# Token-pair loads, halved inversions and transposes by DMA in a delta-rule attention and MLP kernel

## The chip, the cores and the metric

The kernel runs on one core of one Trainium2 chip. The metric is the device time of one execution in microseconds (us), as a median over runs. A profile is one execution; its span, from the first to the last instruction, is some 2 us shorter than the time of the same run. Engines: PE is TensorE (PEld its weight loads), DVE is VectorE, ACT is ScalarE, POOL is GpSimd, SP is SyncE, which here only issues DMAs. A run is called slow when it is over 1.5% above the fastest run of the same kernel, and fast otherwise; intervals and ratios use fast runs alone.

## The reference, cut to what matters

Four batches, eight heads, 768 tokens, head width 48. A recurrence over tokens keeps one 48x48 state per batch and head, and its gated readout is the input of an MLP.

```python
k_n = k / (np.linalg.norm(k, axis=-1, keepdims=True) + 1e-06)
for t in range(S):
    readout = einsum('bhd,bhde->bhe', q[:, :, t], state)
    y[:, :, t] = g[:, :, t] * readout
    v_old = einsum('bhde,bhd->bhe', state, kt)
    state = state + bt * einsum('bhd,bhe->bhde', kt, vt - v_old)
...
x = y.transpose(0, 2, 1, 3).reshape(B * S, H * D)        # 3072 x 384
h = x @ w_in                                             # 384 -> 2048
out = (h * sigmoid(beta * h)) @ w_out                    # 2048 -> 384
```

## The kernel before

The tokens are cut into 12 chunks of 64. For each chunk there is a preparation that no other chunk is needed for (scale k, transpose k and q, products of k and q, the inverse of a triangular 64x64 matrix by repeated products), a short chain that needs the state of the chunk before (pW, w, pU, u, pO, S), then the gated output y, its transpose xT, and the MLP on 256 tokens. The program is planned in Python: every piece of work is an operation with a duration and a key, and a list scheduler puts all of them into one fixed order per engine. On the chip the order is kept; an operation whose input is late holds up everything behind it on that engine.

The transposes, all on TensorE, with a copy out of PSUM (the accumulation memory) after each:

```python
def e_tr(e, sl, dst, src):
    ...
    for s in sl:
        for j in range(PAIRS):
            nc.tensor.transpose(pv[:, s, j, :], sv[:, s, j, :], I128b)
...
G.add(f"pk{c}", [("pe", PAIRS * 57.0 * m)], lambda e, sl=sl: e_tr(e, sl, pk, kp), key - 55, ...)
lean(G.add(f"kT{c}", [("dve", ...), ("act", ...)], lambda e, r=r: e_trc(e, r, kq.t[:, 0, r], pk), ...))
... # pq, qT the same for q
def e_pY(e):
    for s in range(2):
        for i in range(KC):
            nc.tensor.transpose(pv[:, i, s, :], yf[:, s, P * i:P * i + P], I128b)
```

The inverse adds the identity on GpSimd (or DVE) before two of its products:

```python
for sl in groups:
    add_eye(f"ni{c}", ni, nn, K - 37, sl)                # ni = nn + I
...
product(f"pG{c}", pG, ni_, in_j(x4), HJ, HR, SR, ...)
```

The MLP takes chunks in groups; those of two chunks use matmuls of 512 columns:

```python
GROUPS = [[0], [1], [2], [3], [4, 5], [6], [7], [8, 9], [10, 11]]
...
nc.tensor.matmul(ph.t[:, width * i:width * i + width], w_in_b[:, dc, P * fb:P * fb + P],
                 xTb[g].t[:, dc, 0:width], start=(dc == 0), stop=(dc == KC - 1))
```

In gaps the planner puts matmuls of zeros ("fillers") to keep TensorE's clock up. They count as busy time in the profile.

## Time and profile before

| | before |
|---|---|
| median time, 3 runs | 246.2 us (245.78 to 246.34) |
| span of the profile, mean granted clock | 246.8 us, 0.978 (its own run took 248.5 us) |
| first MLP matmul, end of the last one | 31.1 us, 241.2 us |
| PE busy | 221.3 us (90%), 264 transposes of k, q and y among 4930 matmuls |
| DMA busy, first 155 us and after | about 0.9 of 16 engines, then 0.1 to 0.2 |

The page of a profile has the busy shares, then 40 equal slices of the span with a digit for the busy tenths of each, then queues and groups of instructions. A line of the timeline reads: start, duration, engine and source line, operation, output and inputs, shape, count, and in brackets the engine's idle time before it and what released it. "issue" in the brackets means that the profile shows no wait.

### The profile page before, as it was taken

The numbers are of one execution on the slowest core, as the hardware profiler recorded it, in microseconds if no ns is written. First come the engines' busy times: TensorE is split into PE (matmuls) and PEld (weight loads), VectorE is DVE, ScalarE is ACT, GpSimd is POOL, SyncE is SP. The second block draws the span as 40 slices with busy tenths as digits, with TensorE's granted clock in tenths as the row PEclk, the third lists the DMA queues.
The fourth block names the chain that finished last, engine by engine and source line by source line (L and its number), as shares of the span: only waits on it lengthen the run. The fifth ranks groups of instructions, "written<-read, shape, count | busy, mean of one in ns | idle before, by whom it ended". The sixth has DMA issues, their size and how long they took to land.

```text
span 246.8 us, 10951 instructions
## 1 busy us (share of the span) xinstructions
PE 221.3 (90%) x4930; PEld 146.1 (59%) x4950; DVE 157.9 (64%) x208; ACT 170.3 (69%) x287; POOL 124.7 (51%) x110
## 2 busy tenths in 40 slices
PE   4778598786899999999999999999999999999990
PEld 4444475475566776766654657767776456654560
DVE  7568967598657898974797468785893965100000
ACT  4564768596466789868699888778866877357510
POOL 2369447899177976498815874999301002000000
PEclk9999979999599999999999999999999999999999
DMA  6999997969956997998999788703002020020222
GB/s 122 161 206 163 214 241 130 294 104 163 152 90 144 155 189 129 150 163 170 159 176 169 141 159 143 151 5 66 3 13 60 3 66 5 0 66 0 64 64 65
DMA packets 107582, 29.12 MB, mean 118 GB/s; under 512 B 100832, under 2 KB 107504, under 8 KB 107536
## 3 DMA queue, kind: packets, MB, share of 16 engines
q1 hardware_dynamic: 104800, 26.55, 60.7%
q0 software_dynamic: 1600, 1.57, 4.1%
q8 instruction: 38, 0.62, 1.2%
q10 hardware_dynamic: 1136, 0.30, 0.7%
q14 instruction: 8, 0.07, 0.1%
HBM read 25.27 MB, written 4.72 MB: 122 GB/s over the span
## 4 chain that ended last, share of the span: by engine, by line
PE 72%; DVE 8%; DMA 5%; POOL 4%; ACT 4%; issue 3%; ACTq 1%; DVEq 0%; POOLq 0%
PE banks L1159 25%; PE banks L1137 24%; PE banks L743 14%; PE banks L799 4%; PE banks L1025 3%; DMA ld<-in_moe_w_out_dram 3%; DVE w_out_b L737 2%; POOL ni L935 2%; DMA ld<-in_k_dram 2%; PE banks L1108 1%; POOL tiny L827 1%; DVE y L1095 1%; ACT kq L761 1%; ACT raw L761 1%; DVE tt L763 1%
## 5 line engine op out<-in xcount | busy, mean ns | idle before, releaser
L1146 ACT ACTIVATE gT<-banks,betac 128x256 bf16<-128x256 f32 (+1 forms) x144 | 70.0, 550 | 18.3 <-PE banks L1137 18.2
L1159 PE MATMUL banks<-w_out_b,gT 128*128 128x384 bf16 x384 | 74.1, 330 | 4.2 <-DVE w_out_b L737 2.9
L1137 PE MATMUL banks<-xT,w_in_b 128*128 128x256 bf16 (+1 forms) x420 | 71.4, 310 | 2.1 <-ACT gT L1146 0.5
L1137 PEld LDWEIGHTS <-w_in_b 128*128 128x128 bf16 x432 | 40.4, 99 | 21.5 <-issue 2.5
L1159 PEld LDWEIGHTS <-gT 128*128 128x128 bf16 x384 | 34.8, 98 | 24.5 <-issue 4.5
L827 POOL TENSOR_TENSOR tiny<-tiny,half 128x16 f32<-128x16 f32 x10 | 29.3, 2931 | 7.1 <-DVE tiny L820 7.0
L909 DVE TENSOR_TENSOR xa<-banks,UA 128x1024 bf16<-128x1024 f32 x22 | 26.1, 1217 | 4.6 <-PE banks L743 4.5
L763 POOL CAST s<-S_f 64x768 bf16<-64x768 f32 x12 | 9.9, 821 | 30.7 <-DVE S_f L1079 30.2
L761 ACT COPY kq<-banks 128x1024 bf16<-128x1024 bf16 (+1 forms) x21 | 20.4, 974 | 5.3 <-PE banks L799 4.6
L761 ACT COPY ot<-banks 128x384 f32<-128x384 f32 x22 | 10.6, 481 | 18.4 <-PE banks L1159 18.4
L935 POOL TENSOR_TENSOR ni<-l,I64b 128x1024 bf16<-128x1024 bf16 (+1 forms) x10 | 19.4, 1941 | 5.7 <-DVE l L763 5.5
L761 ACT CAST hx<-banks 128x1024 bf16<-128x1024 f32 (+1 forms) x17 | 15.6, 916 | 8.6 <-PE banks L743 8.3
L996 POOL TENSOR_TENSOR vb<-ld,sqt 128x768 f32<-128x768 f32 x12 | 17.7, 1475 | 3.0 <-DMA ld<-in_v_dram 1.8
L972 DVE TENSOR_TENSOR hx<-banks,I 128x1024 bf16<-128x1024 f32 (+1 forms) x13 | 14.6, 1132 | 3.7 <-PE banks L743 3.7
L935 POOL TENSOR_TENSOR ni<-nn,I64b 128x1024 bf16<-128x1024 bf16 (+1 forms) x6 | 11.6, 1938 | 9.0 <-DVE nn L902 8.8
L902 DVE TENSOR_TENSOR nn<-banks,LTn 128x512 bf16<-128x512 f32 x22 | 14.2, 680 | 2.1 <-PE banks L743 2.1
L846 POOL TENSOR_TENSOR kp<-ld,tiny 128x768 bf16<-128x768 f32 x10 | 14.8, 1476 | 0.8
L1035 DVE TENSOR_TENSOR w<-vb,banks 128x768 bf16<-128x768 f32 x11 | 10.5, 951 | 7.0 <-PE banks L1025 7.0
L743 PEld LDWEIGHTS <-ni 64*64 64x64 bf16 x768 | 9.0, 110 | 9.6 <-issue 7.4
L1095 DVE TENSOR_TENSOR y<-banks,ld 128x768 bf16<-128x768 f32 x12 | 11.4, 950 | 2.9 <-PE banks L743 2.9
L1079 DVE TENSOR_TENSOR S_f<-S_f,banks 128x768 f32<-128x768 f32 x10 | 9.5, 951 | 5.7 <-PE banks L743 5.6
L743 PE MATMUL banks<-hx,ni 64*64 64x64 bf16 x768 | 11.8, 197 | 0.9 <-POOL ni L935 0.4
(95 smaller groups left out, 319.4 us busy)
## 6 DMA issues: line engine op xcount, KB each, us to landing
ld<-in_q_dram SPq DMA_DIRECT2D x24, 192.0 KB, 4.9
ld<-in_v_dram SPq DMA_DIRECT2D x24, 192.0 KB, 5.4
ld<-in_g_dram SPq DMA_DIRECT2D x24, 192.0 KB, 5.5
out_dram<-ot SPq DMA_DIRECT2D x24, 192.0 KB, 2.9
ld<-in_k_dram SPq DMA_DIRECT2D x46, 96.0 KB, 4.1
ld<-in_moe_w_out_dram SPq DMA_DIRECT2D x8, 384.0 KB, 6.3
w_in_b<-in_moe_w_in_dram POOLq DMA_DIRECT2D x4, 384.0 KB, 7.6
ld<-in_k_dram ACTq DMA_DIRECT2D x2, 96.0 KB, 4.5
```

The source lines that it names most:

```text
L743: nc.tensor.matmul(out_ps, lhsT, rhs, start=start, stop=stop, tile_position=(C * rows, C * cols), skip_group_check=True)
L761: nc.scalar.copy(o, i)
L827: nc.gpsimd.tensor_tensor(t.t[:, 1, r], t.t[:, 0, r], half[:, r], ALU.pow)
L846: ENG[e].tensor_tensor(kp.t[:, r, :, 0:D], ldk.t[:, r], t.t[:, 3, r, :, None].to_broadcast([P, m, H, D]), ALU.mult)
L902: ENG[e].tensor_tensor(nn.t[:, s].rearrange("p (x j) t -> p x j t", x=2), src.t[:].rearrange("p x (j i t) -> p x j i t", j=PAIRS, i=2)[:, ...
L909: ENG[e].tensor_tensor(xa.t[:, s, :, i, :].rearrange("p (x j) i t -> p x j (i t)", x=2), src.t[:].rearrange("p x (j y) -> p x j y", j=PAIR ...
L935: ENG[e].tensor_tensor(dst.t[:, r].rearrange("p s h t -> p (s h) t"), src.t[:, r].rearrange("p s h t -> p (s h) t"), I64b[:, None, :].to_b ...
L972: nc.vector.tensor_tensor(dst.t[:, r].rearrange("p s h t -> p (s h) t"), src.t[:, r].rearrange("p s (h t) -> p (s h) t", h=H), I64[:, None ...
L996: ENG[e].tensor_tensor(vb.t[:], ldv.t[:], sqt[:, c, :, :, None].to_broadcast([P, 2, H, D]), ALU.mult)
L1137: nc.tensor.matmul(ph.t[:, width * i:width * i + width], w_in_b[:, dc, P * fb:P * fb + P], xTb[g].t[:, dc, 0:width], start=(dc == 0), stop ...
L1146: nc.scalar.activation(gT.t[:, width * i:width * i + width], ph.t[:, width * i:width * i + width], ACT.Silu, scale=betac[:, fb:fb + 1])
L1159: nc.tensor.matmul(acc.t[:, 0:DM], gT.t[:, off + o:off + o + P], w_out_b[:, fb, :], start=(fb == 0), stop=(fb == FB - 1))
```

## The change

The intent: start the chain sooner, and take work from TensorE, which is full from 74 us on, by giving some transposes to the DMA queues. The core of the diff, with cuts marked:

```diff
-GROUPS = [[0], [1], [2], [3], [4, 5], [6], [7], [8, 9], [10, 11]]
+GROUPS = [[0], [1], [2], [3], [4], [5], [6], [7], [8], [9], [10], [11]]
-RAW = (0,)
+RAW = (1,)
+PRE = 40
+SPLIT = (0, 1,)
+EYE = (0, 2,)
+PAIRED_Q = (0, 1, 3,)
+DT_KQ = (4, 5, 6, 8, 9, 10, 11,)
+DT_Y = (6, 8, 9, 10, 11,)
 ... (ORDER of the loads, and a table LEAN of biases for the planner: all new)
-SETS = 3
-AGE = 4000.0
-STAY = 0.0
+SETS = 1
+AGE = 800.0
+STAY = 100.0
 ...
+        if name == "q" and c in PAIRED_Q:
+            for b in range(B):
+                s = src[b, :, C * c:C * c + C, :].rearrange("h (t r) d -> t h (r d)", r=2)
 ...
+        def turn(name, src, i, key):
+            def emit(e):
+                ENG[e].dma_start_transpose(kq.t[:, i].rearrange("p s j t -> p (s j) t"),
+                                           src.t[:].rearrange("p s h d -> p (s h d)"))
+            op = G.add(name, [("sp", 1250.0)], emit, -900 + c, reads=[src], writes=[...], kind="dma")
 ...
+            if c in DT_KQ:
+                turn(f"kd{c}", kp, 0, key - 55)
+            else:
 ...            (pk and kT as before; the same for q, and for y with DT_Y)
-                    mm(quad(dst, b, h, hout[b], slot[b]), lhs(b, h), rhs(b, h), hin[b], hout[b])
+                    mm(o, lhs(b, h), rhs(b, h), hin[b], hout[b], True, not ident)
+                    if ident:
+                        mm(o, I64b[hs(hin[b])], rhs(b, h), hin[b], hout[b], False, True)
```

## The prediction

> **What bounds the kernel now.** I read the busy shares first, then the 40 slices, then the engine times in windows, then the timeline of the first 31 us, and last the queue's own waits. From the page of the kernel before:
>
> ```profile
> PE 221.3 (90%) x4930; PEld 146.1 (59%) x4950; DVE 157.9 (64%) x208; ACT 170.3 (69%) x287; POOL 124.7 (51%) x110
> ...
> PE   4778598786899999999999999999999999999990
> ...
> PEclk9999979999599999999999999999999999999999
> DMA  6999997969956997998999788703002020020222
> ```
>
> The reader is to see two stages. In the first ten slices or so (6.2 us each) PE has gaps; from slice 11 on it is full to the end, while the DMA engines are about nine tenths busy up to slice 25 and then nearly idle. So late PE work costs its whole time, DMA room is plentiful only after 155 us, and early time is a matter of latency. The windows give the size of it (columns: busy time of PE, then the other engines, then granted clock, DMA share, GB/s):
>
> ```profile
> 37.00:49.40 12.40, 10.13 (x329) 6.64 (x328) 8.31 (x10) 8.92 (x19) 9.87 (x8) 1.00 0.92 212
> 49.40:61.70 12.30, 9.73 (x197) 7.50 (x199) 11.03 (x13) 9.57 (x20) 11.94 (x10) 1.00 0.88 133
> 61.70:74.00 12.30, 11.24 (x204) 6.95 (x204) 7.63 (x8) 6.91 (x10) 5.78 (x4) 0.72 0.81 121
> 74.00:86.40 12.40, 12.40 (x364) 9.07 (x361) 9.96 (x11) 8.95 (x16) 10.49 (x8) 1.00 0.83 150
> ```
>
> Between 37 and 74 us PE is idle 2.3 + 2.6 + 1.1 = 6.0 us, and runs partly at a lower clock in the last of the three; from 74 us it has no gap. Before that lies the start. The timeline of the first 31 us shows the path of chunk 0 (start, duration, instruction, idle before and releaser):
>
> ```profile
> 13.67 1.93 ACT L761 CAST raw<-banks 128x1024 bf16<-128x1024 f32 x2 [0.72 <-PE banks L743]
> 14.72 0.69 DVE L909 TENSOR_TENSOR xa<-raw,UA 128x512 bf16<-128x512 bf16 x1 [1.65 <-ACT raw L761]
> ...
> 18.94 1.29 DVE L972 TENSOR_TENSOR hx<-banks,I 128x512 bf16<-128x512 f32 x2
> ...
> 20.72 1.60 POOL L935 TENSOR_TENSOR ni<-nn,I64b 128x512 bf16<-128x512 bf16 x1
> 22.38 0.44 PE L743 MATMUL banks<-hx,ni 64*64 64x64 bf16 x16 [0.42 <-POOL ni L935]
> ...
> 26.33 0.44 PE L743 MATMUL banks<-u,xa 64*64 64x48 bf16 x32
> ...
> 28.95 0.94 DVE L1095 TENSOR_TENSOR y<-banks,ld 128x768 bf16<-128x768 f32 x1
> ```
>
> Here PE waits for GpSimd's addition of the identity, and y of chunk 0 starts 2.2 us after its product is done. The first MLP matmul comes at 31.1 us. The end is pure MLP: 64 matmuls of 384 columns in 10.41 us, then copy and store.
>
> **What the Trainium skill says.** "VectorE: DVE Perf Modes", section "The three transpose paths", gives 390 ns for a 128x128 transpose on TensorE and 1309 ns by DMA. The trace differs on the first: eight transposes start at 116.38 and the next work starts at 116.83, so in a row one costs 56 ns. No run yet shows the second. "DMA: Bandwidth & Descriptors", "Latency and other measured facts", gives 261 GB/s for a DMA transpose with a non-contiguous middle dimension; nothing here shows it either. The same page, "Specifications", puts the smallest transfer at full rate at 512 B; this case has 100832 of 107582 packets under that, and moves 29.12 MB in about 155 us of full DMA work (63% of 246.8), 188 GB/s. "TensorE: Matmul & The Clock Gate", "What's actually happening", says that the clock opens after about 3.4 us of sustained work; the trace agrees: fillers of 512 columns take 430 ns at 7 us and 236 ns at 14 us (8 in 1.89 us).
>
> **The change, part by part.**
>
> Transposes by DMA. For seven chunks (4, 5, 6, 8 to 11) k and q lose 16 PE transposes, for five chunks y loses 6: 7 x 16 + 5 x 6 = 142 of 264, at 56 ns = 8.0 us of PE. All lie in the full stage after about 60 us, where nothing else fills their place, so I count all of it. Their copies go too: 14 of about 1.0 us (ACT) or 0.67 (DVE), and 5 of 0.8, some 16 us of ACT and DVE, off the path. Added: 14 DMAs of 256 KB and 10 of 96 KB, 4.65 MB. At the skill's 261 GB/s that is an estimated 18 us of queue, at this kernel's 188 GB/s 25 us. The queue's 155 us become about 175 to 180, and still end before the last chunk is needed: chunk 11's xT is copied at 214.6 us, with some 26 us of MLP behind it.
>
> Start. Chunk 0 adds the identity inside the PE product, so the wait goes: the second half could start when the two DVE instructions end (18.94 + 1.29 = 20.23) rather than at 22.38, 2.1 us. The raw copy moves to chunk 1: DVE's first reading starts about 1 us earlier, though its reads from PSUM cost as much as these 0.69 us. If y comes at half its delay, 1.1 us more. Sum 4.2 us. q in token pairs has 384 B runs in place of 192 B, for three chunks; but a weight load is now ahead of q0 and halves of the rearranged copy are slower (not the 0.5 ns per element of the plain one), so I count nothing. The 40 matmuls ahead warm the clock; they run while everything waits for k. Of 4.2 us I keep 3, because the chain of waits shows PE held by w_out's cast from 57.74 to 63.16 us, and w_out's last piece now comes behind four more loads.
>
> Middle. Chunk 1 by halves, the new order of loads, casts moved off DVE and a denser filling of gaps aim at the 6.0 us of idle and some 1.5 us lost to the half clock near 66 us. I count 3 of 7.5, a choice and not a measurement.
>
> Costs. The identity products of chunk 2 add 64 small matmuls, two sets of 32 at 0.27 us: 0.5 us. (Chunk 0's fall in idle time.) The new rules go over to small matmuls as soon as one set is ready, where three were waited for. A change of shape costs 0.1 us: six 256-column matmuls alone take 0.76 us, in a run of twelve 1.31 / 2 = 0.66. Ten more round trips cost 2 us. Splitting the paired groups leaves the PE time (six of 256 columns 0.65 us, three of 512 0.65) and adds ACT work: 96 activations of 256 columns for 48 of 512, about 10 us, less than what the lost copies give back.
>
> Sum: 3 + 8.0 + 3 - 0.5 - 2 = 11.5 us off; 246.2 - 11.5 = 234.7 us.
>
> **Rivals.** First, DMA becomes the bound. At 1309 ns for each of 142 blocks one after the other (the skill's figure, taken as a rate) the queue would gain 186 us and the end would go past 260 us. For it: the DMA share is 0.9 until 150 us, exactly where chunks 4 to 6 are turned, and a transpose in SP's queue holds the loads behind it until kp is ready. Against it: sixteen DMA engines share the blocks, the description says that there is room, and chunks have 20 to 30 us of lead at the end. A mild form, all loads 20 us later and the chain just in time, would give 238 to 242. Second, the start's gain is hidden: w_out's cast near 60 us stays the anchor, and only the PE work counts. That is 8.0 - 2.5 = 5.5 us, 240.7 us. The DMA wait of 7.0 us for w_out in the chain of waits speaks for it. Third, the new order does better than I count: all 4.2 at the start, 6 in the middle, no more shape changes: 246.2 - 4.2 - 8.0 - 6 + 0.5 = 228.5 us. The visible idle and half-clock stretches allow it. Fourth, ACT becomes the bound through shorter activations. With 170.3 + 10 - 13 us it does not, though a last chunk alone runs eight pairs of activations of 0.86 us, 6.9 us, beside 10.4 us of matmul.
>
> **Range and chances.** The PE work saved is the firm part, 8.0 less 0.5 to 2.5; the rest is order and latency. From the third rival (228.5, and a little below) to the mild form of the first gives 227 to 242. Within 2% means above 241.3 us, which needs the start hidden and some loss as well: 0.12. Slower by over 2% needs the queue to be the bound: 0.04. Faster by over 2%: 0.84.
>
> **What would show it.** In the profile after: TensorE transposes fall from 264 to 122; no GpSimd addition stands in chunk 0's path, and the first MLP matmul is near 27 to 28 us; PE is full from 70 us or earlier; the DMA share stays high until about 180 us with PE still at 9 there; xT of chunk 11 is there at least 11 us before the end. Wrong if PE shows gaps after 100 us released by a DMA into kq or xT, if SP sits long on waits for kp, or if the first MLP matmul is early but PE then waits for w_out until the same 63 us.

## The result, and the profile after

The changed kernel took 239.17 us (median of 4 runs, 238.79 to 239.78) against 245.99 us of the kernel before (4 runs). The ratio is 0.9729, with a 95% interval of 0.9697 to 0.9761. Ratios here are the mean time of one kernel's fast runs over that of the other's in the same rounds, so not quite the ratio of the medians. It is faster by 6.8 us, where 11.5 were predicted.

The page of the changed kernel, the lines that answer to those of before:

```profile
PE 217.2 (91%) x5132; PEld 154.2 (65%) x5141; DVE 154.5 (65%) x214; ACT 156.8 (66%) x317; POOL 134.6 (57%) x117
...
PE   7597979799999999999999999799997999999991
...
PEclk9997999999999999999999999999999999999999
DMA  5999985998989998999899969989769760404022
```

A slice is 5.95 us. PE is nearly full from the ninth slice on and has two new dents, the sevens in the 26th and the 31st slice (149 to 155 us and 178 to 184 us). From the eighth slice on the DMA engines stay at six tenths or more up to the 33rd, about 196 us; before, they were done at some 160 us. By the landings in the traces, the last load arrives at 197.3 us in place of 160.8. ACT lost 13.5 us of busy time although it has 48 more activations: many copies of transposes are gone.

The windows of the changed kernel, busy time of PE first:

```profile
37.00:49.40 12.40, 10.75 (x292) 8.03 (x293) 9.75 (x14) 10.02 (x22) 9.30 (x8) 1.00 0.98 192
49.40:61.70 12.30, 11.93 (x203) 8.68 (x203) 9.72 (x13) 11.80 (x26) 11.59 (x11) 1.00 1.02 202
61.70:74.00 12.30, 12.30 (x394) 7.85 (x388) 8.90 (x12) 7.26 (x10) 10.18 (x8) 1.00 1.07 170
...
148.00:172.80 24.80, 22.73 (x675) 16.67 (x673) 18.79 (x21) 16.80 (x35) 14.21 (x11) 1.00 1.01 146
172.80:197.40 24.60, 22.95 (x510) 16.08 (x509) 15.90 (x19) 15.88 (x33) 13.06 (x11) 1.00 0.80 135
```

The same late windows of the kernel before:

```profile
148.00:172.80 24.80, 24.39 (x691) 18.19 (x692) 18.85 (x25) 19.37 (x34) 20.62 (x16) 1.00 0.49 91
172.80:197.40 24.60, 24.49 (x579) 16.41 (x580) 19.11 (x22) 18.74 (x33) 3.22 (x4) 1.00 0.08 20
```

In the middle, PE's idle time between 37 and 74 us went from 6.0 to 2.0 us, and the half clock is gone. Part of that is not the change: the profiled run of the kernel before took 248.5 us, 2.3 us above its median, and other runs of it had mean granted clocks up to 0.999, where this profile has 0.978. Late, PE now stands idle for 2.07 + 1.65 = 3.7 us where before it lost 0.5, and in the same windows the DMA share is 1.01 and 0.80 in place of 0.49 and 0.08. But no wait of PE from 148 to 200 us is put down to a DMA. The longest are a break inside a run of equal products and one wait for DVE:

```profile
153.16 0.41 PE L773 MATMUL banks<-nn,xa 64*64 64x64 bf16 x27
155.19 0.24 PE L773 MATMUL banks<-nn,xa 64*64 64x64 bf16 x5 [1.61 <-issue]
...
181.56 0.44 PE L773 MATMUL banks<-u,kp 64*64 64x48 bf16 x32 [0.67 <-DVE u L793]
```

The start is the surprise. The timeline of the changed kernel:

```profile
14.51 0.82 POOL L883 TENSOR_TENSOR kp<-ld,tiny 128x384 bf16<-128x384 f32 x1
...
30.00 0.25 PE L773 MATMUL banks<-u,kp 64*64 64x48 bf16 x8
31.14 0.38 PE L773 MATMUL banks<-u,kp 64*64 64x48 bf16 x24 [0.89 <-issue]
...
31.87 0.96 DVE L1160 TENSOR_TENSOR y<-banks,ld 128x768 bf16<-128x768 f32 x1 [1.01 <-PE banks L773]
...
34.81 1.47 PE L1211 MATMUL banks<-xT,w_in_b 128*128 128x256 bf16 x12
```

The first MLP matmul starts at 34.8 us, 3.7 us later than before, not 3 to 4 us earlier. The GpSimd additions are gone from chunk 0, but its second half of k is now scaled by GpSimd at 14.51 us, behind other work, where DVE had done it at 10.91. The run of 32 products that ends the chain of chunk 0 is broken in the middle by 0.89 us for which the profile shows no wait; e8 comes back to such breaks.

The transposes themselves, as the profile lists DMA issues (count, median us from issue to landing):

```profile
xT<-y SPq DMA_TRANSPOSE x10, 2.3
kq<-kp SPq DMA_TRANSPOSE x7, 4.5
kq<-qp SPq DMA_TRANSPOSE x7, 4.3
```

To see where time went I counted the finished MLP work. The number of weight loads of the two MLP lines that started by each moment, each counted once, times the back-to-back time of one (109 ns for 256 columns, 216 ns for 512, 163 ns for 384), gives this many us of MLP done; the whole is about 125 us.

| done by | 35 us | 50 | 60 | 75 | 100 | 150 | 200 | 230 |
|---|---|---|---|---|---|---|---|---|
| before | 2.0 | 6.5 | 12.9 | 17.6 | 30.7 | 58.6 | 89.1 | 114.4 |
| changed | 0.3 | 5.9 | 11.8 | 19.6 | 35.3 | 66.9 | 97.3 | 122.8 |
| changed, again (e9) | 0.0 | 5.9 | 10.9 | 18.9 | 35.3 | 66.8 | 97.6 | 123.4 |
| e7, chunk 0 first | 2.0 | 5.9 | 11.1 | 18.6 | 32.7 | 62.9 | 96.7 | 122.1 |
| e6, start 3 us later | 0.0 | 5.9 | 8.7 | 17.5 | 32.7 | 64.9 | 96.0 | 120.2 |
| e1, turns on TensorE | 0.3 | 5.9 | 11.8 | 19.3 | 30.3 | 55.6 | 83.0 | 112.7 |
| e8, late turns only | 0.0 | 5.9 | 10.2 | 18.8 | 30.0 | 57.5 | 88.5 | 117.5 |

The changed kernel's lead over the one before is negative up to 60 us, 2.0 us at 75, 4.6 at 100, 8.3 at 150, 8.2 at 200 and 8.4 at 230. So almost all of the gain arises between 60 and 150 us, and the lead is level after it: the new idle time late probably eats what the transposes still save there. The lead at the end is more than the 6.8 us of the medians because the profiled run of the kernel before lies 2.3 us above its median.

### The profile page after: what moved, and what is told of

Its sections match the earlier page's. It is cut to its first block, busy times and chain, and to the rows that moved or that the text cites.

```text
span 237.9 us, 11418 instructions
## 1 busy us (share of the span) xinstructions
PE 217.2 (91%) x5132; PEld 154.2 (65%) x5141; DVE 154.5 (65%) x214; ACT 156.8 (66%) x317; POOL 134.6 (57%) x117
## 4 chain that ended last, share of the span: by engine, by line
PE 52%; DMA 11%; DVE 9%; SPq 7%; POOL 7%; ACT 7%; issue 5%; ACTq 1%; DVEq 0%; POOLq 0%
PE banks L1211 18%; PE banks L1233 15%; PE banks L773 11%; DMA ld<-in_k_dram 5%; SPq L584 4%; DMA xT<-y 3%; ACT gT L1220 3%; PE banks L1266 3%; POOL tiny L864 2%; DMA ld<-in_v_dram 2%; PE banks L1090 2%; DVE xa L966 2%; SPq L1172 2%; PE banks L836 1%; SPq L1249 1%
## 5 line engine op out<-in xcount | busy, mean ns | idle before, releaser
L1220 ACT ACTIVATE gT<-banks,betac 128x256 bf16<-128x256 f32 x192 | 77.2, 479 | 20.5 <-PE banks L1211 19.5
L1211 PE MATMUL banks<-xT,w_in_b 128*128 128x256 bf16 x576 | 73.7, 273 | 1.2 <-ACT ot L791 0.6
L1211 PEld LDWEIGHTS <-w_in_b 128*128 128x128 bf16 x576 | 52.9, 98 | 12.0 <-issue 1.8
L1233 PEld LDWEIGHTS <-gT 128*128 128x128 bf16 x384 | 34.9, 98 | 19.3 <-issue 0.5
L992 POOL TENSOR_TENSOR ni<-nn,I64b 128x1024 bf16<-128x1024 bf16 (+1 forms) x11 | 21.8, 1984 | 16.2 <-DVE nn L959 16.1
L966 DVE TENSOR_TENSOR xa<-banks,UA 128x1024 bf16<-128x1024 f32 (+1 forms) x24 | 26.9, 1126 | 2.6 <-PE banks L773 2.6
L793 DVE CAST hx<-banks 128x1024 bf16<-128x1024 f32 (+1 forms) x15 | 15.6, 1042 | 7.5 <-PE banks L773 7.5
L959 DVE TENSOR_TENSOR nn<-banks,LTn 128x512 bf16<-128x512 f32 x22 | 15.1, 686 | 6.9 <-PE banks L773 6.9
L883 POOL TENSOR_TENSOR kp<-ld,tiny 128x768 bf16<-128x768 f32 (+1 forms) x12 | 16.4, 1366 | 3.3 <-DVE tiny L871 2.6
L1266 PE MATMUL banks<-zeros 128*128 128x512 bf16 x56 | 15.6, 384 | 0.7 <-issue 0.5
L857 DVE TENSOR_REDUCE tiny<-ksq 128x16 f32<-128x768 f32 (+1 forms) x14 | 11.5, 829 | 6.8 <-ACT ksq L848 6.3
L992 POOL TENSOR_TENSOR ni<-l,I64b 128x1024 bf16<-128x1024 bf16 (+1 forms) x8 | 15.1, 1882 | 1.0 <-DVE l L793 0.8
L848 ACT ACTIVATE ksq<-ld 128x768 f32<-128x768 f32 (+1 forms) x12 | 8.8, 739 | 5.3 <-DMA ld<-in_k_dram 5.3
```

What stands on the lines that cost most here:

```text
L793: ENG[e].tensor_copy(o, i)
L883: ENG[e].tensor_tensor(kp.t[:, r, :, 0:D], ldk.t[:, r], t.t[:, 3, r, :, None].to_broadcast([P, m, H, D]), ALU.mult)
L966: ENG[e].tensor_tensor(xa.t[:, s, :, i, :].rearrange("p (x j) i t -> p x j (i t)", x=2), src.t[:].rearrange("p x (j y) -> p x j y", j=PAIR ...
L992: ENG[e].tensor_tensor(dst.t[:, r].rearrange("p s h t -> p (s h) t"), src.t[:, r].rearrange("p s h t -> p (s h) t"), I64b[:, None, :].to_b ...
L1220: nc.scalar.activation(gT.t[:, width * i:width * i + width], ph.t[:, width * i:width * i + width], ACT.Silu, scale=betac[:, fb:fb + 1])
L1233: nc.tensor.matmul(acc.t[:, 0:DM], gT.t[:, off + o:off + o + P], w_out_b[:, fb, :], start=(fb == 0), stop=(fb == FB - 1))
```

## The experiments

My theory, as it stood before these runs: the gain is the TensorE work of the transposes; the start gave nothing, since what follows it is the limit there; the full queue gives part back late. The rivals: the new order makes the gain and the transposes are neutral; the start passes through to the end; the queue has room.

Twelve kernels ran, four at a time beside runs of the kernel before, and all gave correct results. The kernel before spread more than at first (240.9 to 250.7 us), and many of its runs were slow. So the ratios of e1 to e4 have wide intervals, and I give medians and spans as well. The last two columns say how much slower a kernel is than the changed one, in us. "By fast runs": its ratio divided by that of the changed kernel (0.9729 for e1 to e8, 0.9728 for e9 to e12), less 1, times 239 us. "By medians": the same with its median over the median of before in the same call (of the changed kernel 239.17 / 245.99, in the last call 238.76 / 244.46); this mixes fast and slow runs.

| run | median | before beside it | ratio, 95% interval | span of profile | slower, by medians | by fast runs |
|---|---|---|---|---|---|---|
| e1 turns on TensorE | 251.96 | 246.93 | 1.033 (1.014 to 1.052) | 247.9 | 11.8 | 14.8 |
| e2 turns in the old kernel | 260.45 | 246.93 | 1.066 (1.042 to 1.090) | 255.1 | 20.3 | 22.9 |
| e3 pairs back | 248.74 | 246.93 | 1.026 (1.008 to 1.044) | 246.2 | 8.6 | 13.0 |
| e4 turns twice | 259.26 | 246.93 | 1.058 (1.026 to 1.091) | 257.9 (slow) | 19.1 | 20.9 |
| e5 no biases | 239.42 | 244.67 | 0.977 (0.969 to 0.985) | 238.5 | 1.5 | 1.1 |
| e6 start later | 244.58 | 244.67 | 0.995 (0.989 to 1.001) | 240.4 | 6.7 | 5.4 |
| e7 start first | 239.15 | 244.67 | 0.978 (0.971 to 0.985) | 238.6 | 1.3 | 1.3 |
| e8 late turns only | 246.38 | 244.67 | 1.012 (1.009 to 1.016) | 243.4 | 8.5 | 9.7 |
| e9 changed again | 238.76 | 244.46 | 0.973 (0.967 to 0.978) | 237.2 | 0 | 0 |
| e10 outputs on TensorE | 241.82 | 244.46 | 0.987 (0.983 to 0.992) | 240.4 | 3.1 | 3.6 |
| e11 old early part | 246.81 | 244.46 | 1.004 (1.000 to 1.008) | 246.1 (slow) | 8.1 | 7.8 |
| e12 other places | 240.07 | 244.46 | 0.977 (0.971 to 0.983) | 238.7 | 1.3 | 1.1 |

**e1: all transposes back on TensorE, the rest of the change kept.**

```diff
-DT_KQ = (4, 5, 6, 8, 9, 10, 11,)
-DT_Y = (6, 8, 9, 10, 11,)
+DT_KQ = ()
+DT_Y = ()
```

> The changed kernel with all 24 DMA transposes given back to TensorE (DT_KQ and DT_Y empty), everything else of the change kept and the order planned anew by the kernel's own rules. Theory A (the gain is the 8.0 us of TensorE transposes that were taken away, and the rest of the change comes out near zero): 239.2 + 8 = about 247, no faster than the kernel before. Theory B (the queue gives part of it back: PE waited 3.6 us between 148 and 197 us with the queue full): 8.0 - 3.6 = 4.4 us slower, about 243.5. Theory C (the new order makes the gain and the DMA transposes are neutral): 238 to 240.

Its span is 10.0 us longer than the changed kernel's; it is 11.8 us slower by the medians and 14.8 by the fast runs. Rival C falls: without the DMA transposes the new order is no better than the old one; it is even slower than the kernel before. The 142 transposes are worth somewhat more than their 8.0 us of TensorE time. In the table nearly the whole difference arises after 75 us (122.8 - 112.7 = 10.1 us at 230, 0.3 at 75). e1 also shows the price on the other side: with nothing turned in the queue its last load lands at 154.8 us in place of 197.3, and y of chunk 11 comes 15.1 us sooner than in the changed kernel. Here is that y in e1, then in the changed kernel:

```profile
197.65 0.96 DVE L1160 TENSOR_TENSOR y<-banks,ld 128x768 bf16<-128x768 f32 x1 [0.82 <-PE banks L773]
212.78 0.96 DVE L1160 TENSOR_TENSOR y<-banks,ld 128x768 bf16<-128x768 f32 x1 [0.76 <-PE banks L773]
```

**e2: the transposes by DMA put into the kernel before, nothing else.** Groups, order, rules, start and early part are all set back; the two tuples stay.

> The kernel before, with only the 24 DMA transposes added (paired groups, old order of loads, old rules, old start), order planned anew by its own rules. Theory A: 246.0 - 8 = about 238. Theory B with crowding: 241 to 243. Theory D (the transposes need the rest of the change, because they delay the loads and so the last chunk, and the paired last group of 21 us of MLP then starts late): no gain or a loss, 246 to 256, with y of chunk 11 later than 213 us by as much as the kernel is slower.

It lost 13.5 us against the kernel before by the medians, 8.3 by the spans, and its ratio of fast runs is 1.066. That is what theory D expected. The timeline of e2:

```profile
223.54 2.12 PE L1257 MATMUL banks<-zeros 128*128 128x512 bf16 x9
228.88 10.53 PE L1202 MATMUL banks<-xT,w_in_b 128*128 128x512 bf16 x48 [3.23 <-DMA xT<-y]
239.25 10.56 PE L1224 MATMUL banks<-w_out_b,gT 128*128 128x384 bf16 x64
```

y of chunk 11 came at 223.7 us, 10.7 us later than in the kernel before, and PE filled with zeros and then waited for the last transpose. Behind it stood the whole pass of chunks 10 and 11, 21 us. So the transposes by DMA are not a gain by themselves. That single groups alone would turn this loss into a gain is not shown: the kernel before with transposes by DMA and single groups was not run.

**e3: the paired groups put back into the changed kernel.**

```diff
-GROUPS = [[0], [1], [2], [3], [4], [5], [6], [7], [8], [9], [10], [11]]
+GROUPS = [[0], [1], [2], [3], [4, 5], [6], [7], [8, 9], [10, 11]]
```

> The changed kernel with the old groups (chunks 4 and 5, 8 and 9, 10 and 11 share an MLP pass). In the changed kernel y of chunk 11 comes at 212.8 us and the MLP ends 20 us later. With the last two chunks in one pass the MLP behind it is at least 21 us, so the last xT becomes the end's anchor. Theory D: slower by 4 to 10 us (243 to 249), PE idle before the last pass. Theory A (PE work alone counts, groups cost the same PE time): 239 to 240.

Slower by 8.3 us in the span, 8.6 by the medians and 13.0 by the fast runs; its four runs, 247.9 to 251.0 us, agree with theory D or lie somewhat above it. "PE idle before the last pass" shows up as fillers:

```profile
217.56 2.97 PE L1266 MATMUL banks<-zeros 128*128 128x512 bf16 x13
220.37 10.52 PE L1211 MATMUL banks<-xT,w_in_b 128*128 128x512 bf16 x48
230.73 10.56 PE L1233 MATMUL banks<-w_out_b,gT 128*128 128x384 bf16 x64
```

The last pass of 21 us begins at 220.4 us, after y of chunk 11 at 215.1. In the changed kernel y of chunk 11 comes at 212.8 us, but half of that pass is done by then. Single groups save no work; they make it harmless that the last chunk is late, which the transposes by DMA bring about (e1 against the changed kernel: 197.7 and 212.8 us).

**e4: each transpose of k and q issued twice, in the very order of the changed kernel.**

```diff
                 ENG[e].dma_start_transpose(kq.t[:, i].rearrange("p s j t -> p (s j) t"), ...)
+                ENG[e].dma_start_transpose(spare, src.t[:].rearrange("p s h d -> p (s h d)"))
```

(The order of the changed kernel was recorded and replayed, and the unused half of the xT tiles given up for the spare tile.)

> The changed kernel in its very order of instructions, with each of the 14 transposes of k and q issued a second time into a spare tile (3.67 MB more through the same queue, no more TensorE work). If the queue has room: within 1 us of 239.2. If the queue is what made PE wait between 148 and 197 us: 14 more at 1.5 to 2.3 us each are 20 to 30 us of queue, and the kernel is slower by 5 to 25 us, with the new PE gaps after 100 us.

Some 20 us slower (19.1 by the medians, 20.9 by the fast runs); its fast runs, 256.08 and 258.58 us, show it too. Fourteen more transposes cost about 20 / 14 = 1.4 us each. The queue has no room for them: y of chunk 11 came at 232.6 us. What the queue of the changed kernel carries is about what can be hidden. This is a doubling, and does not say that the last few transposes of the changed kernel cost 1.4 us each.

**e5: the planner's table of biases emptied.** A control for how much an order by chance is worth.

> Control: the changed kernel with its table of scheduling biases emptied, everything else kept, so that the same work comes in another order. It says how much of a difference between two planned orders is the chance of the order. If the tuned biases carry the gain: slower by 5 us or more (over 244 on a chip where the kernel before takes 246). If the order is worth little: within 2 us of the changed kernel, 237 to 241.

1.5 us slower by the medians, 1.1 by the fast runs, 0.6 us in the span. So the tuned table carries nearly nothing, and a difference of 3 us or more between two planned orders is more than this one sample of chance. It is one sample only.

**e6: 3 us of empty work put ahead of chunk 0, in the order of the changed kernel.**

```diff
             def e_ks(e, r=r, t=t):
+                if c == 0 and r.start == 0:
+                    for _ in range(4):
+                        nc.vector.memset(spare, 0.0)
```

> The changed kernel in its very order of instructions, with 3 us of empty VectorE work put ahead of the scaling of chunk 0's k, so that the first MLP matmul starts about 3 us later (34.8 to 37.8 us). If the start passes through to the end: 3 us slower, 242.2. If the start is hidden by what comes after (the prediction's second rival): less than 1 us slower.

The first MLP matmul moved from 34.8 to 38.4 us, the span grew by 2.5 us, and y of chunk 1 by 4.7 us (49.9 to 54.6). By the medians it lost 6.7 us, by the fast runs 5.4, but this kernel's runs spread from 240.2 to 247.5 and only 4 of 20 counted as fast, so I take no more from it than that a delay of the whole early chain passes through.

**e7: chunk 0 first.** Biases of -60 for all of chunk 0's operations, its second half of k on DVE, no identity products in chunk 0, the late beta transposes not tied to it.

```diff
-EYE = (0, 2,)
+EYE = (2,)
-            alts = [("dve", dve_sb(384 * m)), ("pool", pool_tt(384 * m))] if c < 2 else ...
+            alts = [("dve", dve_sb(384 * m))] if c < 1 else ...
```

> The changed kernel with chunk 0 put first: its operations biased ahead of all others, its second half of k scaled on VectorE, no identity products in chunk 0, the late beta transposes not tied to it; order planned anew. The first MLP matmul should come 3 to 5 us earlier than 34.8 us. If the start passes through: 234 to 236. If it is hidden, or was traded for chunk 1 and 2: 238 to 241.

This is the test of the start. The source line of the first MLP product in e7 (duration minimum, median, maximum in ns, then the first and last start):

```profile
L1185 PE MATMUL banks<-xT,w_in_b x576: 269/273/284, 31.1 to 228.2; 128*128 128x256 bf16 x192
```

The first MLP matmul is 3.7 us earlier than in the changed kernel, and the time is 239.15 us, no better (1.3 us slower by the fast runs). The table shows where it went: at 50 us every version in it has done 5.9 to 6.5 us of MLP, whether it began at 31.1, 34.8 or 38.4 us. That is the first half of chunk 0's MLP (5.2 us) and a little of its second half, and the rest waits for w_out and for chunk 1, whose y comes at 49 to 50 us in both kernels. With e6, which delayed chunk 1 too, this fits an early stage that is set by the second chunk and not by the first MLP matmul. It is not a clean test: e7's order was planned anew, it is 2.6 us behind the changed kernel in finished MLP work at 100 us, and whether a start that leaves the rest alone would pay stays open.

**e8: only the late k and q turned by DMA (8 to 11), chunks 4 to 6 on TensorE.**

```diff
-DT_KQ = (4, 5, 6, 8, 9, 10, 11,)
+DT_KQ = (8, 9, 10, 11,)
```

> The changed kernel with k and q of chunks 4, 5 and 6 given back to TensorE, those of 8 to 11 and the five outputs still turned by DMA; planned anew. TensorE gets 6 x 8 x 56 ns = 2.7 us more work; if only TensorE work counts: 242. If the six transposes in the full part of the queue cost as much as they save (they delay the loads of chunks 7 to 11): 238 to 240.

A miss for both theories: not even, and not 2.7 us slower, but 5.5 us in the span, 8.5 by the medians and 9.7 by the fast runs. So the transposes in the full part of the queue are not the poor ones; by this run they are worth two to three and a half times their TensorE time. I looked for the reason in the waits of PE. Between 75 and 125 us, e8 has this line:

```profile
PE banks L773 <- issue: 2.9, 4, 1.1
```

In the changed kernel in the same stretch:

```profile
PE banks L773 <- issue: 0.2, 1, 0.2
```

These are breaks inside runs of equal products, such as this one of e8:

```profile
75.78 0.39 PE L773 MATMUL banks<-u,xa 64*64 64x48 bf16 x28
76.88 0.22 PE L773 MATMUL banks<-u,xa 64*64 64x48 bf16 x4 [0.71 <-issue]
```

PE stops after 28 of 32 with no wait in the profile. But from 31 to 200 us the changed kernel, e8 and e1 have about the same of them, in this order:

```profile
PE banks L773 <- issue: 3.4, 5, 1.6
PE banks L773 <- issue: 3.8, 6, 1.1
PE banks L773 <- issue: 3.0, 4, 1.6
```

The breaks lie elsewhere in the changed kernel, and are not fewer. PE's whole idle time from 31 to 200 us is 8.1 us there, 8.0 in e8 and 9.5 in e1. So breaks do not explain the loss of e8, and its cause stays open.

What the breaks are, the kept traces show. "Runtime: NRT & Kernel Launch", section "Instruction fetch mechanics", says that an engine's instructions come in blocks of 16 KiB by a DMA queue of its own, a cost "mostly hidden". The profile's instruction queue moved 0.66 MB in 40 packets in the changed kernel, 16.5 KB each, which agrees. I numbered PE's matmuls and weight loads in each of the 14 traces. All 58 breaks (longer than 0.15 us, after 20 us, not before a filler) come at a number that repeats every 256: 193 or 194 past a multiple of 256 in the twelve experiments' traces, 181 to 188 in the two traces from which a few records are missing. And each ends 1.2 to 2.0 us after an instruction packet has been moved, the n-th packet at the n-th such number. So PE waits there for its next instructions. No run here tried to shorten these waits.

**e9: the changed kernel again,** as the reference.

> Control: the changed kernel itself once more, on the chip that times the other three runs of this call, because the kernel before has spread from 240.9 to 249.3 us on the last two chips. Expected: ratio to the kernel before 0.965 to 0.982, as at first (0.973), and with that the reference for the runs beside it.

Ratio 0.9728, as at first.

**e10: the five outputs transposed by TensorE, k and q by DMA.**

```diff
-DT_Y = (6, 8, 9, 10, 11,)
+DT_Y = ()
```

> The changed kernel with the five outputs turned by TensorE again (30 transposes at 56 ns, 1.7 us), k and q still by DMA; planned anew. If only TensorE work counts: 1.7 us slower than the changed kernel. If the queue is what makes PE wait 3.6 us between 148 and 197 us, ten fewer transposes in just that stretch give 1 to 3 us of it back: even, or up to 1.5 us faster, and the PE idle time there falls below 1 us.

3.1 us slower by the medians and 3.6 by the fast runs, 1.4 to 1.9 more than the TensorE work. PE's idle time between 175 and 200 us fell from 1.4 us (e9) to 0.1, as the queue theory said, but between 125 and 150 it rose from 0.3 to 1.9. So ten transposes fewer moved the late idle time and did not remove it. And it does not need fewer transposes to go away: e5 and e7 turn all 24 by DMA, with DMA shares of 0.81 to 1.23 in the windows from 148 to 197 us, and PE is idle there for 0.72 and 0.85 us, where the changed kernel has 3.7. So the late gaps belong to the one order and its breaks, and not to a full queue as such; their going gained nothing either. The windows of e5:

```profile
148.00:172.80 24.80, 24.21 (x639) 17.91 (x625) 19.53 (x21) 17.85 (x40) 14.94 (x10) 1.00 1.23 148
172.80:197.40 24.60, 24.47 (x581) 17.22 (x580) 17.37 (x22) 17.11 (x36) 12.47 (x12) 1.00 0.81 140
```

**e11: the early part undone, transposes by DMA and single groups kept.**

```diff
-RAW = (1,)
-PRE = 40
-SPLIT = (0, 1,)
-EYE = (0, 2,)
-PAIRED_Q = (0, 1, 3,)
+RAW = (0,)
+PRE = 0
+SPLIT = (0,)
+EYE = ()
+PAIRED_Q = ()
```

> The changed kernel without its early part: no token pairs of q, chunk 1 not by halves, no identity in the product, the raw copy in chunk 0 and not in chunk 1, no matmuls ahead; transposes by DMA, single groups, loads and rules as changed; planned anew. The lead of the changed kernel in finished MLP work at 75 us is 2.2 us. If the early part made it: 2 to 3 us slower than the changed kernel. As the prediction counted (3 at the start and part of 3 in the middle): 4 to 6 us slower. If the early part is worth nothing: within 1 us.

Another miss: 8.1 us slower by the medians, and 7.8 us by the ratios of fast runs (1.0044 / 0.9728), more than any of the three expected. Its fast runs average 245.1 us against 238.5 of e9. The early part is worth more than the lead that it makes by 75 us. Which of the five settings does it stays open, and with 9 of 22 runs fast the size is rough; token pairs alone take 3,072 of 6,144 packets out of the q loads of three chunks, in a queue of which e4 says that it has no room.

**e12: other places for the transposes.** k and q of chunks 5, 7, 8, 10 and 11, y of 4, 5, 6, 9, 10 and 11, token pairs in chunks 0 to 3, the raw copy in chunk 0, AGE 400, STAY 400, EVAC 10, an almost empty table of biases.

> An attempt at a better version, with what the runs showed: k and q turned by DMA for five chunks (5, 7, 8, 10, 11) in place of seven, outputs for six (4, 5, 6, 9, 10, 11), so 80 + 36 = 116 transposes in place of 142 and about 1.1 MB less in the full queue; raw copy in chunk 0, token pairs in four chunks, other rules for the order. PE work is 26 x 56 ns = 1.5 us more. If the queue's load is worth more than that: 236 to 238, 1 to 3 us faster than the changed kernel; if only PE work counts: 1.5 us slower.

1.3 us slower by the medians, 1.1 by the fast runs, ratio 0.9771 against 0.9728 with overlapping intervals. It does not beat the changed kernel, and no version here does.

## Why the prediction was right or wrong

The measured 239.2 us lies in the range, and the forecast of over 2% faster was right, but partly by luck: the start, 3 us of the sum, gave nothing, and the transposes gave more than was counted.

**The TensorE work of the transposes** was the firm part, 8.0 us, less 2 for their round trips. Without it the gain is gone (e1), as predicted, and the size was low: e1 gives 9.8 us between 75 and 230 us by finished MLP work, 10.0 by span and 14.8 by the fast runs. Where the excess comes from stays open; breaks of the instruction stream are not it (e8).

**The costs** beside the round trips were sized at 0.5 us. e1 has the transposes where the kernel before has them, and between 75 and 230 us it does 93.4 us of MLP against 96.8: the rest of the change costs 3.4 us in that stretch. The two profiles' runs are not at their kernels' medians (249.8 of 252.0 us, 248.5 of 246.2), so this is rough. The 2 us for round trips had no working, and no run measures them alone.

**The start** is the step that failed: "Of 4.2 us I keep 3". The identity wait did go, but the first MLP matmul came at 34.8 us and not at 27 to 28, because the plan let chunk 0's second half stand behind GpSimd's other work. And a start of 31.1 us gained nothing in e7. The second rival ("the start's gain is hidden") named the anchor as w_out's cast near 60 us. In the table all versions meet earlier, at 50 us, where y of chunk 1 is due as well. The reading for that anchor was too long: from 57.74 to 63.16 us the cast stood in the chain of waits, but PE itself was idle for it only 1.9 + 1.1 = 2.9 us.

**The middle** was counted at 3 us, a choice. Start and middle together were to give 6 us; the lead at 75 us is 2.0 us (1.3 in the repeat). So by these profiles some 4 us of the 4.7 us by which the sum was too high (11.5 against 6.8) sit here. Idle time fell by 4.0 us between 37 and 74, but fillers, which count as busy, took part of its place: 9 of them, 3.4 us, before and 12, 4.5 us, after. Also, the half clock that was to be saved belonged to the profiled run, and the fastest run of the kernel before had almost none of it (240.9 us, mean clock 0.999).

**The first rival in its mild form** was partly right: the last load lands at 197 us and not at the predicted 175 to 180. The 24 DMAs take more of the queue than the 18 to 25 us of the prediction: the last load lands 36.5 us later than in the kernel before, and 42.5 later than in e1, waits for the inputs of the transposes included. One term was misread: 188 GB/s divided all of the 29.12 MB by 155 us, stores after that time included; up to 155 us the trace has 164 GB/s. The prediction said that the last chunk has 20 to 30 us of lead. y of chunk 8 came 7.8 us sooner than before, of chunk 9 5.4, of chunk 10 1.4 and of chunk 11 0.2 us (212.8 and 213.0), so the queue did eat the lead of the last chunks; e4 shows how near the edge that is. The sign of PE gaps after 100 us that a DMA ends did not come: PE has new gaps of 3.7 us between 148 and 197 where 0.5 were, none put down to a DMA. The strong form, 1309 ns for each block one after another, is wrong: it would have made 186 us of queue.

**Not seen at all** was that the parts need each other. By themselves the transposes lose 13.5 us by the medians (e2), and without single groups the changed kernel loses 8.6 (e3). Taking back the transposes (e1), the single groups (e3) or the early part (e11) each costs more than the whole gain of 6.8 us, so no share of the gain can be given to one part alone. The prediction listed the split of the groups under costs, as neutral for PE; it is what lets the late last chunk be hidden. It also counted nothing for the token pairs and the forty matmuls, while the early part as a whole is worth some 8 us in the changed kernel (e11).

The third and fourth rivals did not come: ACT's busy time fell to 156.8 us.

## What to carry to other kernels

Work moved from a full engine to a queue pays only while whatever the queue feeds last still has slack; look for the largest indivisible piece of work behind that last arrival, and cut it, before moving anything. An earlier start need not be worth anything while the second thing that the stage waits for is no earlier: compare the finished work of the bound engine at several times, not the time of its first instruction. Before a gap is called the reason of a loss, sum such gaps over the whole run in both kernels: they may only have moved. When parts of a change lean on each other, undo each of them in the changed kernel and also add it alone to the old one; the two answers differed here by tens of microseconds.

## What the Trainium skill lacked or had wrong

- "VectorE: DVE Perf Modes", "The three transpose paths": 390 ns on TensorE is no rate. Eight in a row cost 56 ns each here, and 142 of them, with what hangs on them, were worth 9.8 to 14.8 us (e1), 69 to 104 ns each.
- The same table's 1309 ns by DMA for 128x128 is neither a rate nor a latency of larger transfers: one DMA of eight such blocks landed in 4.3 to 4.5 us, one of three in 2.3 us, and with the queue full eight more blocks cost about 1.4 us (e4), 0.18 us a block.
- "DMA: Bandwidth & Descriptors", "Latency and other measured facts", gives 261 GB/s for a transpose with a non-contiguous middle dimension. 256 KB in 1.4 us is 183 GB/s by the time that it costs in a full queue (e4), and 4.65 MB in the 42.5 us by which the last load lands later than in e1 is 109 GB/s, waits for the inputs of the transposes included; no run measured a transpose alone.
- "Runtime: NRT & Kernel Launch", "Instruction fetch mechanics", calls the fetch mostly hidden. Here the changed kernel stood 3.4 us in such waits between 31 and 200 us, the longest 1.6 us, and e11 had one of 2.1. I found no page that says how to see it: a break with "issue" inside a run of equal matmuls, at the same place in every 256 instructions of PE, 1.2 to 2.0 us after an instruction packet.
- I found no page that says that an order fixed in advance turns a late DMA into idle time of the bound engine: in e2 the last pass of 21 us waited 3.2 us for the last transpose.
